# Retention and two gated MLPs on one core: a product kept in PSUM, subtractions moved to GpSimd, stores behind loads, chunks reversed, ten conversions moved up

## Chip, core and metric

One core of one Trainium2 chip. The metric is the device time of one launch in microseconds (us), lower is better. The core has five engines with instruction streams of their own: TensorE (PE, its weight loads PEld), VectorE (DVE), ScalarE (ACT), GpSimd (POOL) and SyncE (SP), which issues most DMAs. Each stream runs in its program order; streams wait for each other by semaphores.

## The reference

Three stages on 4 x 768 tokens of width 512, all in float32:

```python
for t in range(S):                        # retention, 8 heads of 64
    state = gamma * state + outer(k_t, v_t)
    y_t = scale * q_t @ state
h = x @ w_in;  x = (h * cos(h)) @ w_out   # first MLP, 512 -> 2048 -> 512
h = x @ w_in2                             # second MLP, same sizes
g = where(h >= 1, h, where(h <= -1, 0, (h + 1)**2 / 4))
out = g @ w_out2
```

The second MLP's weights arrive as 64-bit words that the kernel converts to float32.

## The kernel before

Every float32 matrix is split into a high part, rounded to the matmul's format, and a low part, the remainder (`high_part`, ACT; `low_part`, POOL). A product is three matmuls: high x high, low x high, high x low.

**Stage 1, first MLP.** Six blocks of 512 tokens; hidden chunks of 128, 16 of them, in two halves of eight (k = 0 and k = 1). A step is `first` (12 matmuls) for one chunk and `second` (12 matmuls) for the chunk three steps earlier; `act` puts the cosine between them. There are 96 steps. Retention runs beside the first 40 of them, block 5 of k = 0 is steps 40 to 47, and k = 1 is steps 48 to 95, eight to a block. When a block is done, `evacuate` (L573) moves four accumulator banks out: even ones with an addition on DVE (L578), odd ones with a copy on ACT (L582) and an addition on POOL (L584). The next block's accumulation takes the same banks.

**Conversion.** `Convert` turns one [128 x 512] weight slice of 64-bit words into float32: load of the raw words (L146), two DVE passes (L153, L156), one on ACT (L161), a DVE pass (L167), a POOL addition (L174). `Conveyor` gives each slice one method per step (`one`, `two`, ...), by lag. The first MLP's slices are converted early. All 32 slices of the second MLP's weights (m = 1) are converted in k = 1, in three steps of four. Two neighbouring slices make a pair: `combine` (L190) forms four half-width sums of it on POOL (L211), and `part` (L213) splits four pieces, the low parts with a DVE subtraction (L225), and stores them on SP at once (L228, L229). From step 68 on, `right_sides(0)` also forms and splits the right-hand sides of stage 2, one closure a step.

**Stage 2, second MLP.** `Products` uses a 2 x 2 block scheme with seven products in place of eight (names 11, t1, 21, t2, 22, t3, t4). Token blocks go in three pairs (p = 0, 1, 2), each with eight groups g % 8, 24 groups in all, with one more pass to drain. In `group` (L859) there are seven segments; each has one input `product` (6 matmuls, L737) of this group and one `output` (6 matmuls, L753) of the group before. The ramp is ACT (`ramp`, `square`) and DVE (`larger`, L789). `add` (L792) adds a finished output bank y to an SBUF accumulator (L823); an output's matmuls wait until its y bank is read. Seven activations per group are split: four direct ones and three differences (t1, L995; t2, L1019; t3, by `minus`), with t4 at L915; low parts are formed by `low` (L779), some on POOL, some on DVE. In segment E the group's d bank receives a sum, its activated value goes to an SBUF tile (`take(g, "22")`).

While p = 0 and p = 1 run, `tick` (L883) calls one closure of `right_sides(p + 1)` five times a group, groups 2 to 6 of each pair: 8 subtractions (L651) and 14 splits (L698), then stores. Two of the five calls use DVE, three POOL. Weight tiles of each group come from DRAM by `load` (L615) on SP, eight a group, and `load_x` fetches the next right-hand sides at a pair's end. When a pair is done, its four accumulators are transposed by DVE (L831) and `send` (L847) issues 16 small DMAs in a row on SP, twice. At the very end two of the four accumulators go by TensorE transposes (L807) and copies (L813, L815), the other two by DVE and 16 small DMAs, half on the ACT queue.

Of the kernel before, what the change touches and what calls it, by code (L numbers as in the profile page):

```python
# [40 lines left out]
def tile_retention_mlp_mlp(  # L41
# [25 lines left out]
    NWARM = 10  # L67

# [5 lines left out]
    yq_d = dram.tile([P, NP, TB], F32, name="yq")  # L74
    w32_d = {
        (m, j, a): dram.tile([P, TB], F32, name=f"w32_{m}_{j}_{a}")
        for m, j, a in [(0, j, a) for j in range(NH, NF) for a in range(2)]
# [56 lines left out]
    class Convert:  # L134
# [4 lines left out]
        def __init__(self, m, j, a, keep):  # L139
            self.m, self.j, self.a, self.keep = m, j, a, keep  # L140

        def load(self, stage):
            self.stage = stage
            self.raw = self.stage.tile([P, TB, 2], I32, tag="raw", name="raw", bufs=3 - self.m)
            src = (w1, w2)[self.m][self.j][:, self.a * TB:(self.a + 1) * TB]
            nc.sync.dma_start(out=self.raw.rearrange("p n w -> p (n w)"), in_=src.bitcast(I32))  # L146

        def one(self):
            ncs, ncf = ((3, 3), (1, 5))[self.m]
# [10 lines left out]
        def two(self):  # L160
            nc.scalar.activation(  # L161
                out=self.s, in_=self.raw[:, :, 0].bitcast(U32), func=AF.Copy, scale=2.0 ** -29
            )

        def three(self):
            f = self.f.bitcast(I32)
# [5 lines left out]
        def four(self):  # L172
            f = self.f.bitcast(I32)
            nc.gpsimd.tensor_tensor(out=f, in0=f, in1=self.s, op=ALU.add)  # L174

        def five(self):
# [3 lines left out]
            elif self.m == 1:  # L180
# [32 lines left out]
        def part(self, n):  # L213
# [9 lines left out]
            for x, o in self.pieces[n]:  # L223
                w = x.shape[-1]
                nc.vector.tensor_tensor(  # L225
                    out=x.bitcast(F32R), in0=x, in1=hi[:, o:o + w].bitcast(F32), op=ALU.subtract
                )
                nc.sync.dma_start(out=to[:, 1, o:o + w], in_=x)  # L228
            nc.sync.dma_start(out=to[:, 0, :], in_=hi[:, :wide[n]].bitcast(F32))  # L229

        def seven(self):
            if self.m == 1 and self.j % 2:
# [3 lines left out]
        def eight(self):  # L236
            if self.m == 1 and self.j % 2:
# [3 lines left out]
    left = {}  # L241

    class Conveyor:
# [20 lines left out]
        def advance(self):  # L264
            if self.late:
                order = (("five", 2), ("one", 1), ("two", 1), ("three", 1), ("four", 1), ("seven", 3), ("eight", 4))
# [321 lines left out]
    class Products:  # L588
# [7 lines left out]
        def __init__(self):  # L596
            self.w, self.x, self.f, self.g = {}, {}, {}, {}
            self.spare, self.ready = [], []
            self.done, self.turned = {}, {}
            self.queue = [[], []]  # L600
            self.eng = nc.gpsimd
# [12 lines left out]

        def load(self, a, g, n):  # L615
            if g >= self.NG:
                return
# [4 lines left out]
            nc.sync.dma_start(out=t.bitcast(F32), in_=wp_d[a][g % NH][n])  # L622
# [13 lines left out]
        def release(self, a, g, n):  # L636
            self.slots[a].append(self.w.pop((a, g, n))[0])
# [43 lines left out]
        def remake(self, p):  # L681
# [12 lines left out]
            def parts(c, q):  # L694
# [3 lines left out]
                self.eng.tensor_tensor(out=lo, in0=x[c][q], in1=hi.bitcast(F32), op=ALU.subtract)  # L698
# [31 lines left out]
        def product(self, g, q, to, begin):  # L730
# [10 lines left out]
            if g % NH == NH - 1:  # L741
                self.free_x(p, q)
                n = 2 * ORDER.index(q)
                for m in range(NP + n, min(NP + n + 2, 14)):
# [15 lines left out]
        def take(self, g, q):  # L760

            if q == "21":
                t = tp.tile([P, TB], F32, tag="r", name="r", bufs=5)
            else:
                nm = {"11": "h6", "t3": "h6", "t1": "l6", "t4": "l6", "22": "h7", "t2": "l7"}[q]
                pool = self.tmp if q == "t3" else wpool[0]
                t = pool.tile([P, TB], F32, tag=f"wo{nm}", name=f"f{q}")
# [20 lines left out]
        def larger(self, r, h):  # L788
            nc.vector.tensor_tensor(out=r, in0=h, in1=r, op=ALU.max)  # L789


        def add(self):  # L792
# [10 lines left out]
            elif fine and final and n == 0:  # L803
                for e in range(2):
                    nc.vector.tensor_tensor(out=a[:, e, :], in0=y[:, e, :], in1=a[:, e, :], op=ALU.add)
                    for i, z in enumerate(self.z[h]):
                        nc.tensor.transpose(z[:, e * P:(e + 1) * P], a[:, e, i * P:(i + 1) * P], self.eye)  # L807
                for i, z in enumerate(self.z[h]):
                    o = tp.tile([P, TB], F32, tag="r", name="o", bufs=5)[:, :2 * P]
                    to = o.rearrange("p (k e b) -> p e k b", k=4, e=2)  # L810
                    src = z.rearrange("p (e k b) -> p e k b", k=4, e=2)
                    if i < 2:
                        nc.vector.tensor_copy(out=to, in_=src)  # L813
                    else:
                        nc.scalar.activation(out=to, in_=src, func=AF.Copy)  # L815
                    t0 = (i * NC + 2 * p) * C
                    rows = out[t0:t0 + C, :].rearrange("t (k x) -> t k x", k=4)
                    (nc.sync, nc.scalar)[h * (i // 2)].dma_start(
                        out=rows[:, :, h * 64:(h + 1) * 64], in_=o.rearrange("p (k x) -> p k x", k=4)
                    )  # L820
# [9 lines left out]
            def turned():  # L830
# [3 lines left out]
                if at in (("22",) if fine else ("12", "21")):  # L834
                    self.send(p, n, fine)

            if fine:
                turned()
            else:
                self.turned[at] = turned  # L840
# [6 lines left out]
        def send(self, p, n, fine):  # L847
# [3 lines left out]
            for k in range(4):  # L851
                src = t[32 * k:32 * (k + 1)].rearrange("p (q c) e -> p q c e", q=NP)
                for q in range(NP):
                    (nc.scalar if fine and q % 2 else nc.sync).dma_start(
                        out=rows[k, :, q, 2 * p + n, :, :], in_=src[:, q]
                    )


        def group(self, g, banks, ends):  # L859
# [3 lines left out]
            if live:  # L863
                a, b, c, d = [bank(i) for i in banks]
# [18 lines left out]
            def tick(eng=nc.gpsimd):  # L883
                if self.ready:
                    self.eng = eng
# [16 lines left out]
            if live:  # L902
                self.product(g, "11", a, True)
            self.add()
            if o:
                self.square(o["r21"])
                self.larger(o["r21"], o["h21"])
            if live:
                s1 = copy(a)
            if o:  # L910
# [5 lines left out]
                self.low(prev, "22")  # L916
# [6 lines left out]
            if live:  # L923
                self.product(g, "t1", b, True)
# [12 lines left out]
            if live:  # L937
                tick(nc.vector)

            if live:  # L940
                self.product(g, "21", c, True)
# [21 lines left out]
            if live:  # L963
                s6 = copy(a)
                self.square(r11)
                self.larger(r11, c)
# [13 lines left out]
            outputs("t3", y0, False)  # L980
            done(2, 2)
# [8 lines left out]
            if live:  # L990
                plus(d, a, s5)
                self.square(r12)
                self.larger(r12, b)
# [6 lines left out]
            outputs("21", y1, True)  # L1000
            done(0, 3)
            if live:
                tick(nc.vector)
            if live and g % NH == NH - 2:
                for n in range(NP):
# [6 lines left out]
            if not fine:  # L1012
                self.add()
# [11 lines left out]
            outputs("t4", y0, False)  # L1025
            if prev >= 0:
                self.release(1, prev, 3)

        def run(self, before):
# [13 lines left out]
            for g in range(self.NG + 1):  # L1043
# [7 lines left out]
                if g == self.NG:  # L1051
                    self.z = [bank(i) for i in banks]
                    self.z = [[t[:, o:o + 2 * P] for t in self.z[2 * h:2 * h + 2] for o in (0, 2 * P)] for h in range(2)]
# [359 lines left out]
```

## Time and profile before

| | |
|---|---|
| median of 3 runs | 1173.91 us (1169.13 to 1176.9) |
| the profiled execution, its own time | 1170.15 us |
| its span | 1168.4 us |
| TensorE busy, of the span | 1098.0 us, 94% |
| VectorE | 891.6 us, 76% |
| ScalarE | 610.4 us, 52% |
| GpSimd | 554.8 us, 47% |
| mean granted TensorE clock | 0.985 |
| chain that ended last | PE 57%, DVE 16%, DMA 9%, issue 7%, POOL 6% |

A busy TensorE is one with matmuls in its pipe, not one at its peak; so the number of matmuls in a stretch is read beside the busy time. The span leaves out what lies around the first and last instruction; here that is 1.75 us.

### The profile page before, as it was taken

Reading aid. Unit: us, or ns where it says so; the run is one execution under the profiler, and the core shown is the slowest. Engines: PE = TensorE matmul, PEld = TensorE weight load, DVE = VectorE, ACT = ScalarE, POOL = GpSimd, SP = SyncE. Lnnn points to the kernel's source line nnn. Section 1 sums busy time; section 2 is a strip of 40 time slices with the busy share of each in tenths; the row PEclk is TensorE's granted clock in tenths of the full one; section 3 lists DMA queues with packets and bytes.
Section 4 is the critical chain, followed back from the end, with each engine's and each line's share of the span. In section 5 each row is a group of like instructions: output and inputs, shape, how many; then the busy total and the mean of one; then the engine's idle time right before and its main releaser. Section 6 shows DMA issues by size and latency. Waiting matters only on the chain.

```text
span 1168.4 us, 16673 instructions
## 1 busy us (share of the span) xinstructions
PE 1098.0 (94%) x5758; PEld 885.6 (76%) x5758; DVE 891.6 (76%) x1149; ACT 610.4 (52%) x1090; POOL 554.8 (47%) x441
## 2 busy tenths in 40 slices
PE   8999999999999999979889998989988989999995
PEld 5787888888888887868778786767776767778883
DVE  6877566654335789798996589888979888988986
ACT  3554233333345545555554575666555666566662
POOL 4735223321045355666662446756336756345542
PEclk9999999999999999989999999999999999999998
DMA  9476375833173878878776676789697889686543
GB/s 359 158 232 271 111 276 191 298 127 144 46 295 122 291 257 273 302 244 303 276 230 245 227 236 226 261 266 394 203 294 235 267 270 393 202 271 199 180 146 81
DMA packets 125909, 274.63 MB, mean 235 GB/s; under 512 B 17152, under 2 KB 46464, under 8 KB 121856
## 3 DMA queue, kind: packets, MB, share of 16 engines
q1 hardware_dynamic: 119152, 254.94, 64.2%
q10 hardware_dynamic: 6672, 18.61, 4.4%
q8 instruction: 46, 0.75, 0.3%
q14 instruction: 39, 0.32, 0.1%
HBM read 192.76 MB, written 80.74 MB: 234 GB/s over the span
## 4 chain that ended last, share of the span: by engine, by line
PE 57%; DVE 16%; DMA 9%; issue 7%; POOL 6%; ACT 4%; SPq 1%; ACTq 0%; DVEq 0%; POOLq 0%
PE b L567 15%; PE b L480 13%; PE b L737 12%; PE y L753 12%; DMA wo<-wp 2%; DMA raw<-in_w 2%; DVE s L225 2%; DVE cf L225 2%; POOL big L698 2%; PE b L359 1%; PE b L411 1%; DVE cf L153 1%; DVE cf L156 1%; DVE b L532 1%; PE b L417 1%
## 5 line engine op out<-in xcount | busy, mean ns | idle before, releaser
L174 POOL TENSOR_TENSOR cf<-cf,cs 128x512 int32<-128x512 int32 x64 | 86.8, 1356 | 187.8 <-DVE cf L167 113.0
L523 DVE SCALAR_TENSOR_TENSOR r<-b,r 128x512 f32<-128x512 f32 x96 | 65.8, 685 | 130.1 <-ACT r L518 130.1
L518 ACT ACTIVATE r<-b 128x512 int32<-128x512 f32 x96 | 56.8, 591 | 192.1 <-PE b L480 165.0
L567 PE MATMUL b<-gh,wo 128*128 128x512 f32 x384 | 102.9, 405 | 17.5 <-DVE o L578 17.5
L823 DVE TENSOR_TENSOR xh<-y,xh 128x1024 f32<-128x1024 f32 x89 | 108.0, 1213 | 7.9 <-PE y L753 7.9
L753 PE MATMUL y<-wi,wo 128*128 128x512 f32 x342 | 91.0, 402 | 13.8 <-issue 6.8
L567 PEld LDWEIGHTS b<-gh,wo 128*128 128x128 f32 x384 | 74.9, 196 | 34.7 <-ACT r L529 19.0
L536 ACT ACTIVATE gh<-b 128x512 fp32r<-128x512 f32 x96 | 57.2, 596 | 80.3 <-DVE b L532 80.2
L881 POOL TENSOR_TENSOR ft<-f,r 128x512 f32<-128x512 f32 x24 | 41.8, 1743 | 116.6 <-DVE f L789 116.6
L737 PE MATMUL b<-wih,wi 128*128 128x512 f32 x352 | 94.7, 391 | 0.7 <-DVE b L873 0.7
L480 PE MATMUL b<-xh,wi 128*128 128x512 f32 x384 | 95.0, 389 | 0.0
L753 PE MATMUL y<-wo,wo 128*128 128x512 f32 x324 | 83.9, 394 | 8.5 <-issue 3.5
L753 PEld LDWEIGHTS y<-wi,wo 128*128 128x128 f32 x342 | 64.5, 192 | 32.8 <-issue 12.7
L823 DVE TENSOR_TENSOR xl<-y,xl 128x1024 f32<-128x1024 f32 x65 | 79.0, 1215 | 12.4 <-PE y L753 12.1
L480 PEld LDWEIGHTS b<-xh,wi 128*128 128x128 f32 x384 | 72.4, 189 | 15.2
L567 PE MATMUL b<-gh,woh 128*128 128x512 f32 x192 | 77.3, 408 | 2.8 <-ACT woh L117 2.8
L753 PEld LDWEIGHTS y<-wo,wo 128*128 128x128 f32 x324 | 59.6, 188 | 26.2 <-issue 5.1
L753 PE MATMUL y<-gh,wo 128*128 128x512 f32 x228 | 71.3, 394 | 7.0 <-issue 3.0
L737 PEld LDWEIGHTS b<-wih,wi 128*128 128x128 f32 x352 | 66.3, 189 | 15.2 <-DVE b L873 1.1
L480 PE MATMUL b<-xh,wih 128*128 128x512 f32 x192 | 75.4, 395 | 1.6 <-ACT wih L117 0.9
L480 PE MATMUL b<-xh,wil 128*128 128x512 f32 x192 | 74.3, 390 | 0.0
L567 PE MATMUL b<-gh,wol 128*128 128x512 f32 x192 | 74.0, 390 | 0.0
(146 smaller groups left out, 2787.3 us busy)
## 6 DMA issues: line engine op xcount, KB each, us to landing
wi<-wp SPq DMA_DIRECT2D x72, 512.0 KB, 4.9
wo<-wp SPq DMA_DIRECT2D x72, 512.0 KB, 5.1
raw<-in_w SPq DMA_DIRECT2D x64, 512.0 KB, 5.3
wp<-whi SPq DMA_DIRECT2D x48, 256.0 KB, 3.0
qk<-in_qk SPq DMA_DIRECT2D x23, 512.0 KB, 7.3
wp<-s SPq DMA_DIRECT2D x32, 256.0 KB, 2.1
xTh<-xh ACTq DMA_DIRECT2D x6, 1024.0 KB, 5.6
xTl<-xl ACTq DMA_DIRECT2D x6, 1024.0 KB, 9.6
```

The lines of the kernel that those rows point to most:

```text
L174: nc.gpsimd.tensor_tensor(out=f, in0=f, in1=self.s, op=ALU.add)
L225: nc.vector.tensor_tensor(out=x.bitcast(F32R), in0=x, in1=hi[:, o:o + w].bitcast(F32), op=ALU.subtract)
L480: nc.tensor.matmul(out=h, lhsT=w[:, c * P:(c + 1) * P], rhs=x[:, c, :], start=(i == 0), stop=(i == len(terms) - 1),)
L518: nc.scalar.activation(out=self.r.bitcast(I32), in_=self.h, func=AF.Identity, scale=INV_2PI, bias=0.25)
L523: nc.vector.scalar_tensor_tensor(out=self.r, in0=self.h, scalar=INV_2PI, in1=self.r.bitcast(I32), op0=ALU.mult, op1=ALU.subtract,)
L536: nc.scalar.activation(out=self.gh, in_=self.h, func=AF.Copy)
L567: nc.tensor.matmul(out=acc[k, b][e], lhsT=w[:, s], rhs=g, start=(begin and i == 0), stop=(last and i == 2),)
L698: self.eng.tensor_tensor(out=lo, in0=x[c][q], in1=hi.bitcast(F32), op=ALU.subtract)
L737: nc.tensor.matmul(out=to, lhsT=w[:, c * P:(c + 1) * P], rhs=x, start=begin and n == 0, stop=n == len(terms) - 1, skip_group_check=not begin,)
L753: nc.tensor.matmul(out=to[:, e, :], lhsT=w[:, e * P:(e + 1) * P], rhs=a, start=begin and m == 0, stop=m == 2, skip_group_check=not begin,)
L823: nc.vector.tensor_tensor(out=a, in0=y, in1=a, op=ALU.add)
L881: nc.gpsimd.tensor_tensor(out=o, in0=x, in1=z, op=ALU.subtract)
```

## The change

- `low_part` on POOL forms the low parts of the converted weights; the stores are collected and issued by `send_parts` after the next step's load; `part` 3 and 0 come with 1 and 2.
- Odd accumulators of k = 1 are added on DVE straight from the bank.
- Three conversions move into the retention stretch, seven into block 5 of k = 0; their float32 result goes to DRAM (ACT queue) and is loaded in k = 1 in place of conversion.
- In stage 2, 22's activated value is written over the d bank. t2 and t3 read it there on DVE; t1, the low parts of t1 and t2 and all ticks are on POOL; the low part of 22 is on DVE.
- p = 1 walks its chunks backwards, so the weights of the last group of a pair are kept for the first of the next.
- Row stores go five per segment. The end uses TensorE transposes for all four accumulators and stores whole rows. One pair of buffers is given from the activations to the right-hand sides.

```diff
+    READY = 10
+    FIRST = 3
...
     def load(self, stage):
+            if self.ready:
+                self.f = self.stage.tile([P, TB], F32, tag="cf", name="cf", bufs=5)
+                nc.sync.dma_start(out=self.f, in_=w32_d[self.m, self.j, self.a])
+                return
...
     def part(self, n):
-                nc.vector.tensor_tensor(
-                    out=x.bitcast(F32R), in0=x, in1=hi[:, o:o + w].bitcast(F32), op=ALU.subtract
-                )
-                nc.sync.dma_start(out=to[:, 1, o:o + w], in_=x)
-            nc.sync.dma_start(out=to[:, 0, :], in_=hi[:, :wide[n]].bitcast(F32))
+                low_part(hi[:, o:o + w], x.bitcast(F32R), x)
+                stores.append((to[:, 1, o:o + w], x))
+            stores.append((to[:, 0, :], hi[:, :wide[n]].bitcast(F32)))
...
+    def send_parts():
+        for o, x in stores:
+            nc.sync.dma_start(out=o, in_=x)
+        stores.clear()
...
     def evacuate(done, n):
-            if e % 2 == 0 and add:
+            if add:
                 nc.vector.tensor_tensor(out=o, in0=a, in1=add.pop(0), op=ALU.add)
...
+        def chunk(self, g):
+            p, l = divmod(g, NH)
+            return NH - 1 - l if p % 2 else l
+        def again(self, g):
+            return g > 0 and g % NH == 0
         def load(self, a, g, n):
-            if g >= self.NG:
+            if g >= self.NG or self.again(g):
                 return
...
         def turn(self):
-            for f in self.queue.pop(0):
+            for f in self.queue.pop(0) + self.rows[:5]:
                 f()
+            del self.rows[:5]
...
         def sums(self, x, *which):
-                self.eng.tensor_tensor(out=x[o], in0=x[a], in1=x[b], op=ALU.subtract)
+                nc.gpsimd.tensor_tensor(out=x[o], in0=x[a], in1=x[b], op=ALU.subtract)
...
         def group(self, g, banks, ends):
-                self.low(prev, "22")
+                self.low(prev, "22", nc.vector)
...
-                self.low(prev, "t2", nc.vector)
+                self.low(prev, "t2")
...
-                nc.vector.tensor_tensor(out=t1, in0=r12, in1=r11, op=ALU.subtract)
+                minus(t1, r12, r11)
                 self.low(g, "11")
-                r22 = self.take(g, "22")
+                r22 = r()
                 self.ramp(r22, d)
...
                 self.square(r22)
-                self.larger(r22, d)
+                self.larger(d, r22, d)
                 self.high(g, "t1")
                 t2 = self.take(g, "t2")
-                nc.vector.tensor_tensor(out=t2, in0=r22, in1=t1, op=ALU.subtract)
-                self.low(g, "t1", nc.vector)
-                minus(self.take(g, "t3"), r22, r12)
+                self.less(t2, d, t1)
+                self.less(self.take(g, "t3"), d, r12)
+                self.low(g, "t1")
+                self.f[g, "22"] = d
...
+        def final(self):
+            a, p, h, n = self.finals.pop(0)
...
+            for e in range(2):
+                for i in range(NP):
+                    nc.tensor.transpose(z[i][:, e * P:(e + 1) * P], a[:, e, i * P:(i + 1) * P], self.eye)
...
+            for i in range(NP):
+                t0 = (i * NC + 2 * p + n) * C
+                (nc.sync, nc.scalar)[i // 2].dma_start(out=out[t0:t0 + C, :], in_=self.out[n][:, i, :])
...
     def run():
-                now = 5 <= i < 12 if i < 2 * NH else (i < 3 * NH + 4 or i % 2) and bool(todo)
+                now = 5 <= i < 12 if i < 2 * NH else (i < 3 * NH + 4 or i % 2 or i > 33) and bool(todo)
...
-                conv.start(todo.pop(0) if todo and k == 1 and l % 4 != 3 else None, stage)
+                conv.start(todo.pop(0) if todo and (l < 7 if k == 0 else l % 4 != 3) else None, stage)
                 first(k, b, j, 4 + i % 4)
+                send_parts()
```

## Rows read from the trace of the kernel before

**Rows 1.** Windows, stage 1: length, busy us (x instructions) per engine, clock, DMA share, GB/s.
```profile
310.90:354.40 43.50, 43.50 (x194) 36.02 (x193) 16.76 (x26) 21.46 (x40) 15.30 (x12) 1.00 0.55 206
397.90:441.40 43.50, 43.50 (x194) 36.02 (x193) 36.10 (x49) 20.36 (x40) 23.70 (x21) 1.00 0.78 279
441.40:488.00 46.60, 43.87 (x194) 36.02 (x193) 39.44 (x60) 25.27 (x47) 23.47 (x22) 1.00 0.90 307
488.00:541.40 53.40, 46.24 (x194) 37.71 (x193) 50.40 (x61) 28.77 (x55) 35.90 (x32) 0.90 0.74 249
541.40:590.40 49.00, 45.25 (x194) 37.05 (x193) 44.82 (x57) 26.46 (x50) 31.22 (x26) 0.97 0.82 279
590.40:640.50 50.10, 46.27 (x194) 37.75 (x193) 39.07 (x55) 24.84 (x48) 21.59 (x20) 0.93 0.69 235
```

**Rows 2.** Waits, whole span: engine, line, awaited; total us, times, longest.
```profile
PE b L567 <- DVE o L578: 17.5, 4, 7.2
```

**Rows 3.** Windows, stage 2, four groups each, columns PE, PEld, DVE, ACT, POOL.
```profile
697.40:785.70 88.30, 79.25 (x338) 62.20 (x337) 76.22 (x77) 56.56 (x100) 58.69 (x42) 1.00 0.76 250
785.70:872.40 86.70, 80.23 (x338) 63.29 (x337) 73.42 (x81) 52.53 (x91) 39.14 (x28) 0.98 0.85 293
872.40:960.70 88.30, 79.27 (x338) 62.21 (x337) 76.25 (x77) 56.62 (x100) 58.73 (x42) 1.00 0.79 261
960.70:1044.90 84.20, 78.80 (x338) 62.20 (x337) 73.39 (x81) 52.53 (x91) 39.15 (x28) 1.00 0.86 298
1044.90:1121.00 76.10, 76.10 (x338) 63.00 (x336) 65.73 (x73) 51.55 (x89) 39.22 (x28) 1.00 0.62 195
```

**Rows 4.** Timeline in a group with ticks: start us, us, engine, line, operation.
```profile
722.00 1.73 POOL L881 TENSOR_TENSOR ft<-f,r 128x512 f32<-128x512 f32 x1 [2.42 <-DVE f L789]
722.50 1.79 DVE L779 TENSOR_TENSOR gl<-ft,gh 128x512 fp32r<-128x512 f32 x1
...
724.21 1.21 DVE L823 TENSOR_TENSOR xl<-y,xl 128x1024 f32<-128x1024 f32 x1
...
725.49 0.30 PEld L753 LDWEIGHTS y<-gh,wo 128*128 128x128 f32 x2 [1.57 <-issue]
```

**Rows 5.** Timeline behind the first pair's end, SP queue and TensorE.
```profile
848.48 8.58 SPq L854 DMA_DIRECT2D out<-big  x16
...
861.22 1.19 PE L753 MATMUL y<-wi,wo 128*128 128x512 f32 x2 [3.08 <-DMA wo<-wp]
```

**Rows 6.** Timeline of the end.
```profile
1155.13 0.40 PE L753 MATMUL y<-gl,wo 128*128 128x512 f32 x1
...
1160.35 0.66 ACT L815 ACTIVATE o<-b 128x256 f32<-128x256 f32 x2 [14.52 <-DMA out<-big]
```

**Rows 7.** Groups by line and form, whole span: busy us, mean ns, idle before.
```profile
L174 POOL TENSOR_TENSOR cf<-cf,cs 128x512 int32<-128x512 int32 x64 | 86.8, 1356 | 187.8 <-DVE cf L167 113.0 <-ACT whi L117 22.6 <-issue 16.0
L167 DVE SCALAR_TENSOR_TENSOR cf<-raw,cf 128x512 int32<-128x512 int32 x64 | 58.8, 920 | 1.3
L225 DVE TENSOR_TENSOR s<-s,whi 128x512 fp32r<-128x512 f32 x32 | 37.0, 1196 | 5.2 <-ACT whi L117 4.5 <-issue 0.7
L225 DVE TENSOR_TENSOR cf<-cf,whi 128x256 fp32r<-128x256 f32 x32 | 22.3, 736 | 2.1 <-ACT whi L117 2.1
L120 POOL TENSOR_TENSOR wo<-wo 128x512 fp32r<-128x512 f32 x8 | 10.3, 1293 | 0.9 <-ACT wo L117 0.9
L211 POOL TENSOR_TENSOR s<-cf,s 128x256 f32<-128x256 f32 x16 | 12.2, 762 | 1.3
L995 DVE TENSOR_TENSOR ft<-r,f 128x512 f32<-128x512 f32 x24 | 25.0, 1042 | 2.4
L779 DVE TENSOR_TENSOR wi<-ft,wi 128x512 fp32r<-128x512 f32 x17 | 23.8, 1402 | 0.0
L789 DVE TENSOR_TENSOR r<-b,r 128x512 f32<-128x512 f32 x48 | 32.6, 680 | 6.3 <-ACT r L786 6.3
```

**Rows 8.** Waits of the SP queue, whole span.
```profile
SPq L228 <- DVE s L225: 92.4, 27, 10.6
```

More of the change, by code (lines that the diff above doesn't have):

```diff
@@ L134, in tile_retention_mlp_mlp, with __init__ @@
     class Convert:
[L139 to L140 removed]
+        def __init__(self, m, j, a, keep, late=False, ready=False, store=False):
+            self.m, self.j, self.a, self.keep, self.late, self.ready = m, j, a, keep, late, ready
+            self.store = store or not late
         def load(self, stage):
             self.stage = stage
[L144 removed]
+            if self.ready:
+                self.f = self.stage.tile([P, TB], F32, tag="cf", name="cf", bufs=5)
+                nc.sync.dma_start(out=self.f, in_=w32_d[self.m, self.j, self.a])
+                return
+            self.raw = self.stage.tile([P, TB, 2], I32, tag="raw", name="raw", bufs=3 - self.late)
             src = (w1, w2)[self.m][self.j][:, self.a * TB:(self.a + 1) * TB]
@@ L148, in one @@
         def one(self):
-            ncs, ncf = ((3, 3), (1, 5))[self.m]
+            if self.ready:
+                return
+            ncs, ncf = ((3, 3), (1, 5))[self.late]
             self.s = self.stage.tile([P, TB], I32, tag="cs", name="cs", bufs=ncs)
@@ L160, in two @@
         def two(self):
+            if self.ready:
+                return
             nc.scalar.activation(
@@ L165, in three @@
         def three(self):
+            if self.ready:
+                return
             f = self.f.bitcast(I32)
@@ L172, in four @@
         def four(self):
+            if self.ready:
+                return
             f = self.f.bitcast(I32)
@@ L236, in eight @@
         def eight(self):
-            if self.m == 1 and self.j % 2:
+            if not self.store and self.j % 2:
                 self.part(3)
                 self.part(0)
-    left = {}
+    left, stores = {}, []
+    def send_parts():
+        for o, x in stores:
+            nc.sync.dma_start(out=o, in_=x)
+        stores.clear()
     class Conveyor:
@@ L265, in advance @@
             if self.late:
-                order = (("five", 2), ("one", 1), ("two", 1), ("three", 1), ("four", 1), ("seven", 3), ("eight", 4))
+                order = (("five", 2), ("one", 1), ("two", 1), ("three", 1), ("four", 1), ("seven", 3), ("eight", 3))
             else:
@@ L598, in __init__ @@
             self.spare, self.ready = [], []
-            self.done, self.turned = {}, {}
+            self.done, self.turned, self.out = {}, {}, {}
+            self.rows, self.finals = [], []
             self.queue = [[], []]
-            self.eng = nc.gpsimd
             self.NG = NB // 2 * NH
@@ L636, in release @@
         def release(self, a, g, n):
-            self.slots[a].append(self.w.pop((a, g, n))[0])
+            t = self.w.pop((a, g, n))
+            if self.again(g + 1) and g + 1 < self.NG:
+                self.w[a, g + 1, n] = t
+            else:
+                self.slots[a].append(t[0])
         def right_sides(self, p):
@@ L743, in product @@
                 n = 2 * ORDER.index(q)
-                for m in range(NP + n, min(NP + n + 2, 14)):
+                for m in range(NP + 1 + n, min(NP + n + 3, 14)):
                     self.load_x(p + 1, m)
@@ L802, in add @@
                 nc.vector.tensor_copy(out=a, in_=y)
-            elif fine and final and n == 0:
+            elif fine and final:
                 for e in range(2):
                     nc.vector.tensor_tensor(out=a[:, e, :], in0=y[:, e, :], in1=a[:, e, :], op=ALU.add)
[L806 to L820, printed above, removed]
+                self.finals.append((a, p, h, n))
                 return
@@ L902, in group @@
             if live:
+                a = bank(banks[0])
                 self.product(g, "11", a, True)
@@ L923, in group @@
             if live:
+                b = bank(banks[1])
                 self.product(g, "t1", b, True)
@@ L937, in group @@
             if live:
-                tick(nc.vector)
+                tick()
             if live:
+                c = bank(banks[2])
                 self.product(g, "21", c, True)
@@ L1000, in group @@
             outputs("21", y1, True)
+            self.final()
             done(0, 3)
             if live:
-                tick(nc.vector)
+                tick()
             if live and g % NH == NH - 2:
-                for n in range(NP):
+                for n in range(NP + 1):
                     self.load_x(g // NH + 1, n)
@@ L1052, in run @@
                     self.z = [bank(i) for i in banks]
-                    self.z = [[t[:, o:o + 2 * P] for t in self.z[2 * h:2 * h + 2] for o in (0, 2 * P)] for h in range(2)]
+                    self.nz = 0
                 self.group(g, banks, ends)
@@ L1061, in run @@
                     )
-                    self.pairs += [("wo", n) for n in range(NH + NP + 1, NF)]
+                    self.pairs += [("wo", n) for n in range(NH + NP + 1, NF - 1)]
+                    self.spare.append(self.pair(("wo", NF - 1)))
                     t = [xpool.tile([P, NP, TB], F32R, tag=t, name=t) for t in ("xh", "xl")]
```

83 lines of the change are left out of this document (49 added, 34 removed).

## The prediction, made before the result was known

> **What bounds the kernel now.** I read the windows cut at the blocks of stage 1 and at every four groups of stage 2 first, since the page's shares of busy time mix stages; then the waits of TensorE, then the timeline before single gaps, and last the groups by line, for prices.
>
> A block of eight steps takes 43.50 us when TensorE never waits, with 194 matmuls in it (the first two of [rows 1]). The last four blocks have as many matmuls and take 46.60, 53.40, 49.00 and 50.10 us: 3.1 + 9.9 + 5.5 + 6.6 = 25.1 us lost. In the worst of them the granted clock is 0.90; between the two levels, 2.4 and 1.2 GHz, that is 10.7 us at the lower one, so about half of its 9.9 us is the price of the slow clock after a stop, not of the stop. VectorE is busy 50.40 of 53.40 us there, and the stop itself is TensorE waiting for the evacuation's addition on VectorE, 17.5 us in four waits [rows 2]. VectorE has fallen behind, and the bill is presented at the block's end, when its banks are needed.
>
> Four groups of stage 2 take 76.10 us when TensorE never waits (338 matmuls, 2.72 us a segment; the last of [rows 3]). The four others with that count take 88.30, 86.70, 88.30 and 84.20: 12.2 + 10.6 + 12.2 + 8.1 = 43.1 us lost. The two of 88.30 are those with ticks; VectorE is busy 76.2 us in them, GpSimd 58.7. A typical gap [rows 4]: a GpSimd subtraction starts at 722.00; VectorE's subtraction of two SBUF tiles starts at 722.50 and takes 1.79 us, ending 0.56 us after GpSimd's; the accumulation from y behind it ends at 725.42, and TensorE's load of output weights starts at 725.49. The row says "issue", but the reader is to see that VectorE's queue was the last to finish. In the two windows at the ends of pairs part of the loss is of another kind: 16 row stores hold the SP queue for 8.58 us, and TensorE then waits 3.08 us for a weight tile [rows 5].
>
> The end: the last output matmul is done at 1155.5, the span ends at 1168.4, 12.9 us later, and ScalarE's copies start only at 1160.35, behind the stores on its queue [rows 6].
>
> So at most 25.1 + 43.1 us are in the two stages and some 8 of the 12.9 us in the end, since a last addition, transposes, copies and stores have to remain.
>
> **The change, part by part.**
>
> *Low parts of the weights to GpSimd, odd evacuations to VectorE.* VectorE loses 37.0 + 22.3 us and eight more subtractions of full width at 1.196, 69 us over 16 pairs, 4.3 a pair, 13 a block of three pairs [rows 7]. It gains two additions a block at 0.680. The worst block falls from 50.4 to about 39 busy us; a block in which it was busy 36.10 lost nothing (the second of [rows 1]). GpSimd gains, a pair, 2.5 full subtractions and two half ones: 2.5 x 1.293 + 2 x 0.762 = 4.8, 14.3 a block, and loses two additions (2.6) [rows 7]. Its busy time in the third to fifth block goes from 23.5, 35.9, 31.2 to 35.2, 47.6, 42.9 against 43.5. No stretch of this trace has GpSimd above two thirds, so this is the unknown of the change. Between "all 25.1 us come back" and "none do, GpSimd gates where VectorE did" I take what the sums show: 4 us over in the fourth block, 1 us in its neighbours, and 2 us of lower clock; 18 us come back.
>
> *Stores behind the next load.* The SP queue spent 92.4 us waiting for those subtractions, with the next raw load behind them [rows 8]. Afterwards the stores wait for GpSimd, and behind them are the load after next, the evacuation's stores and the fetch of right-hand sides. A raw load gets one more step, 5.4 us, of slack; I count this into the 18 and nothing on its own.
>
> *Ten conversions earlier.* One costs VectorE at most three passes of 0.920 and GpSimd 1.356 [rows 7]. Seven in the last block of k = 0 raise VectorE from 16.76 to at most 36.1 us of 43.5, which was seen to be free, GpSimd from 15.3 to 24.8 [rows 1]. Three more lie beside the retention, where VectorE has as much room: nothing. If that cover were gone they would cost up to 28 us of VectorE time. The k = 1 blocks that lose them (the first two) lost nothing before, so the gain is nothing either, but the queues enter the third block empty. Ten stores and ten loads of float32 slices are added, 5 MB; the kept weights take away 7 MB.
>
> *22 in PSUM, t1 and low parts on GpSimd, ticks on GpSimd.* Per group VectorE gives up t1 (1.042) and two low parts (about 1.40 each) and takes t3 and the low part of 22 from the bank, at the price of an operation with a bank operand, 0.680 [rows 7]; t2 stays. In tick groups some 1.6 subtractions more go, at 0.68 to 1.4. That is 19.1 - 3.8 - 1.6 + 1.4, about 15 us of 19.0. GpSimd does one operation more, and in tick groups those 1.6: 14.7 + 2.6 x 1.293 = 18.0 at today's durations [rows 3, 7]. They fall if the durations do: of VectorE's operations in the group loop none has two SBUF operands any more, and the 1.73 us of [rows 4] is 0.44 above the 1.293 of one alone. I take 17, again below the segment rate and again above anything shown. The added wait is t2 on VectorE for t1 on GpSimd; queued behind it are t3, the next accumulation and the release of a y bank, which TensorE needs. t1 is issued one segment, 2.72 us, ahead, which covers it when GpSimd has at most one operation in front. Bounds: all 24.4 us of tick groups return, or the new wait costs as much as the old and 8 us on top. I take 17 returned, since the nearest row (the last of [rows 3], VectorE at 65.73 of 76.10 busy and no loss) shows that the loop tolerates one engine at 86%.
>
> The trace shows two neighbours slowed together when both read two SBUF operands [rows 4]. The Trainium skill, page "SBUF — State Buffer", section "SBUF: two separate sides", says why: VectorE and GpSimd share a port pair that one holds for a whole instruction while the other blocks, and a VectorE operation with one bank operand is not among those that take it. By that rule GpSimd's operations in stage 2 fall to 1.29 each, 16 us a tick group, and the stall is gone; by today's durations alone it is 18.
>
> *Chunks reversed, row stores five a segment, spare pair.* Sixteen weight loads vanish at the two turns, just where the next right-hand sides are loaded. 16 stores take 8.58 us of SP [rows 5], 0.54 each; five are 2.7 us, a whole segment, so weight loads still slip by some 0.7 us a segment over seven segments, but none waits 8.58 us. A tile is fetched most of a group ahead. Of 18.7 us in the two windows I take 11 back: the 3.08 with its slow clock, once, and the doubled operations; between 3 and 18.7.
>
> *The end.* Two transposes on VectorE, 16 small stores and the delay of ScalarE's copies go; 16 TensorE transposes come, beside waits. After 1155.5 remain two additions, transposes, copies, issue and landing: about 9 us. 4 us return; between -1 and 8.
>
> Sum: 18 + 17 + 11 + 4 = 50 us from 1170.15, the profiled execution's own time: 1120. That execution lies 3.8 us below the median of the runs shown and inside their spread; I put half of this on it: **1122 us**.
>
> **Rivals.**
>
> *A. GpSimd becomes the bound.* For it: 47.6 of 43.5 us in one block, 17 to 18 of 19.0 in tick groups, and waits of its own for ScalarE's high parts. Against it: with work queued, waits overlap. At 1.73 us for each of 12.4 operations a tick group takes 21.5, no less than 22.1 now: nothing of the 24.4, some 12 of stage 1, 9 of the turns, 4 of the end: 25 us, 1147. The Trainium skill, "GPSIMD Engine Reference", section "Engine selection", advises against GpSimd for two-input work as about 2x slower; the trace agrees for work undisturbed, 1.293 against 0.680 [rows 7], and by that rule this rival is the result.
>
> *B. The SP queue takes over.* Five row stores fill a segment, the weight loads behind them come late and the 3.08 us wait recurs with its clock: the 11 us are not gained: 1133. Against it: sixteen loads fewer at that place.
>
> *C. Slower: t1's wait.* Where a tick's two sums stand before t1 in GpSimd's queue, t1 is 2 x 1.29 + 1.29 late; past the 2.72 us of slack VectorE stops, its accumulations stop, and low parts of t1 and t2 come late the same way. If each of them adds the 3.2 us by which GpSimd's three operations exceed one of 0.68, that is 6.4 us on ten tick groups, 64 us, against 24.4 removed: 40 us lost, 26 kept elsewhere: 1184. It decides from about 5 us a tick group on.
>
> *D. No change.* The stops move to another engine in both stages and the gains of the turns are eaten: 1170.
>
> **How the numbers follow.** A measurement of this kernel tells about 1%, 12 us, from no change. Forecast 0.64, own range 1104 to 1136; A 0.18; B 0.06; C 0.06; D 0.06. The range reaches down to nearly all of the losses returned (25.1 + 43.1 + 4 gives 1098; 1102 taken) and up over A with its bounds to 1158; C, D and a little of both ends are outside. Faster by over 1%: forecast, B and nearly all of A, 0.87. Within 1%: D and a rest of A, 0.07. Slower: C, 0.06.
>
> **What would show it.** Right: third to sixth blocks of k = 1 at 44 to 48 us, the waits for L578's successor under 6 us in total; GpSimd over 40 us busy in a block; tick windows at 77 to 82 us with GpSimd operations near 1.3; no wait of TensorE for weights at the turns; under 10 us after the last output matmul. Wrong: VectorE's idle time before t2 put down to GpSimd's t1; ScalarE waiting for GpSimd's sums in k = 1; TensorE waiting for wp tiles. The forecast fails if GpSimd is late by more than a segment for long stretches.

## The result

The changed kernel takes 1119.42 us, median of the runs timed first, against 1172.3: ratio 0.9543, 95% interval 0.9499 to 0.9587, so 53 us less. Timed again, in five executions, it takes 1116.68 (ratio 0.9542, 0.9521 to 0.9562). The forecast was 1122 in a range of 1102 to 1158. The execution profiled with the first timing was disturbed (2796 us, the common matmul forms at 828 ns on the mean where they take about 390 otherwise) and is left out of the ratios; without it the first median is 1118.84. The rows below are of the same kernel in the later run, an execution of 1114.82 us.

| | before | after |
|---|---|---|
| profiled execution, its span | 1170.15, 1168.4 us | 1114.82, 1113.0 us |
| TensorE busy | 1098.0 us (94%) | 1086.1 us (98%) |
| VectorE busy | 891.6 us | 776.6 us |
| GpSimd busy | 554.8 us | 631.3 us |
| last four blocks of k = 1, sum (174.0 without waits) | 199.1 | 181.6 |
| sixteen groups with losses, sum (304.4 without waits) | 347.5 | 312.5 |

The last two lines are sums of windows: of [rows 1], [rows 3], and of the answer below, with the same columns (length; busy us and count of PE, PEld, DVE, ACT, POOL; clock, DMA share, GB/s). The first four are blocks three to six of k = 1. Then come four times four groups: the first and third hold nearly all ticks ("tick windows"), the second and fourth lie around the ends of pairs ("turn windows"). The last is four groups that waited for nothing before either.

```profile
441.70:485.20 43.50, 43.50 (x194) 36.02 (x193) 29.62 (x45) 22.63 (x43) 33.72 (x33) 1.00 0.88 314
485.20:529.40 44.20, 44.17 (x194) 35.70 (x193) 33.52 (x44) 25.80 (x50) 41.35 (x39) 1.00 0.78 279
529.40:579.80 50.40, 46.12 (x194) 37.66 (x193) 38.51 (x49) 26.84 (x50) 46.53 (x43) 0.93 0.83 293
579.80:623.30 43.50, 43.50 (x194) 35.92 (x193) 27.30 (x40) 22.88 (x44) 28.12 (x29) 1.00 0.70 242
680.80:757.80 77.00, 76.52 (x338) 63.07 (x337) 57.88 (x67) 56.34 (x100) 65.74 (x53) 1.00 0.84 284
757.80:834.40 76.60, 76.39 (x338) 62.94 (x337) 64.62 (x74) 52.11 (x92) 43.07 (x35) 1.00 0.81 273
834.40:915.80 81.40, 78.64 (x338) 63.99 (x337) 57.91 (x67) 55.91 (x100) 65.31 (x52) 0.98 0.85 293
915.80:993.30 77.50, 76.84 (x338) 62.83 (x337) 64.68 (x75) 52.50 (x92) 43.49 (x36) 1.00 0.82 275
993.30:1069.50 76.20, 76.20 (x338) 63.12 (x337) 59.48 (x69) 51.04 (x89) 40.53 (x33) 1.00 0.61 200
```

The reader is to see the exchange of VectorE and GpSimd: in the tick windows VectorE goes from 76.2 to 57.9 us, GpSimd from 58.7 to 65.7, and TensorE loses 0.9 and 5.3 us where it lost 12.2 twice. In stage 1 one block of four still loses, the fifth, 6.9 us, with GpSimd at 46.5 of 50.4.

The groups by line of the changed kernel, against [rows 7]; the last column is idle time before and who ended it:

```profile
L809 POOL TENSOR_TENSOR gl<-ft,gh 128x512 fp32r<-128x512 f32 x56 | 71.8, 1301 | 1.3 <-ACT gh L120 1.3
L920 POOL TENSOR_TENSOR ft<-r,f 128x512 f32<-128x512 f32 x24 | 31.2, 1298 | 140.7 <-PE y L784 93.4 <-DVE r L819 47.3
L954 POOL TENSOR_TENSOR ft<-f,ft 128x512 f32<-128x512 f32 x23 | 30.0, 1303 | 21.0 <-DVE f L819 21.0
L822 DVE TENSOR_TENSOR ft<-b,ft 128x512 f32<-128x512 f32 x24 | 16.6, 692 | 2.5
```

t1 (L920, formerly DVE at 1042 ns), t4 (L954) and the low parts of full width take GpSimd 1.30 us with little scatter; t2 (L822) follows on VectorE after 2.5 us of idle time in all, so the wait that rival C feared hardly exists.

What is left in the fifth block is rival A on a small scale. The timeline there (start, length, engine, operation):

```profile
544.43 0.63 ACT L120 ACTIVATE wih<-wih 128x512 fp32r<-128x512 f32 x1 [4.20 <-POOL wih L682]
...
545.74 1.43 POOL L227 TENSOR_TENSOR s<-cf 128x256 f32<-128x256 f32 x2
547.14 0.73 POOL L227 TENSOR_TENSOR s<-s,cf 128x256 f32<-128x256 f32 x1
...
547.90 0.63 ACT L120 ACTIVATE whi<-s 128x512 fp32r<-128x512 f32 x1 [2.28 <-POOL s L227]
...
550.17 0.57 ACT L537 ACTIVATE r<-b 128x512 int32<-128x512 f32 x1
...
550.78 0.69 DVE L542 SCALAR_TENSOR_TENSOR r<-b,r 128x512 f32<-128x512 f32 x1 [6.92 <-ACT r L537]
...
551.99 2.48 DVE L597 TENSOR_TENSOR o<-b,xh 128x512 f32<-128x512 f32 x4
...
552.81 3.75 PE L586 MATMUL b<-gh,wo 128*128 128x512 f32 x8 [4.28 <-DVE o L597]
```

ScalarE waits for GpSimd twice, 4.20 us for a difference of right-hand sides (L682) and 2.28 us for half sums (L227), each time to make a high part; its next step's rounding (L537) stands behind. VectorE waits 6.92 us for that, and the evacuation behind it holds TensorE. The engine named at TensorE's wait is VectorE, as before; the late one is GpSimd. At the end, the last copies start at 1107.53 and the last store is issued at 1107.95, against copies that start from 1160.35 to 1164.85 before ([rows 6] and the first line here):

```profile
1164.85 0.38 ACT L815 ACTIVATE o<-b 128x256 f32<-128x256 f32 x1 [0.71 <-DMA out<-o]
```

```profile
1107.53 0.66 ACT L893 ACTIVATE big<-b 128x256 f32<-128x256 f32 x2 [1.71 <-PE b L884]
1107.95 0.82 ACTq L898 DMA_DIRECT2D out<-big  x2
```

From the end of the last output matmul (1103.9) to the end of the span are 9.1 us.

### The profile page after: what moved, and what is told of

Its sections match the earlier page's. It is cut to its first block, busy times and chain, and to the rows that moved or that the text cites. A ratio compares the mean times of both kernels' runs of the same rounds, so it can differ in the third digit from the quotient of the medians.

```text
span 2794.4 us, 16654 instructions
## 1 busy us (share of the span) xinstructions
PE 2785.6 (100%) x5774; PEld 1677.8 (60%) x5774; DVE 763.1 (27%) x1053; ACT 606.0 (22%) x1082; POOL 614.7 (22%) x541
## 4 chain that ended last, share of the span: by engine, by line
PE 100%; DVE 0%; ACT 0%; issue 0%
PE b L499 25%; PE b L586 25%; PE b L768 21%; PE y L784 21%; PE b L378 2%; PE b L436 2%; PE b L430 2%; PE b L401 1%; PE b L884 0%; PE b L1157 0%; DVE big L891 0%; DVE b L912 0%; DVE xl L838 0%; ACT xh L120 0%; ACT big L893 0%
## 5 line engine op out<-in xcount | busy, mean ns | idle before, releaser
L537 ACT ACTIVATE r<-b 128x512 int32<-128x512 f32 x96 | 57.3, 597 | 1087.2 <-PE b L499 1046.7
L586 PE MATMUL b<-gh,wo 128*128 128x512 f32 x384 | 244.0, 828 | 0.0
L499 PE MATMUL b<-xh,wi 128*128 128x512 f32 x384 | 239.9, 828 | 0.0
L784 PE MATMUL y<-wi,wo 128*128 128x512 f32 x360 | 228.0, 827 | 0.0
L190 POOL TENSOR_TENSOR cf<-cf,cs 128x512 int32<-128x512 int32 x64 | 81.7, 1276 | 608.5 <-DVE cf L181 403.6
L768 PE MATMUL b<-wih,wi 128*128 128x512 f32 x320 | 211.2, 828 | 0.0
L784 PE MATMUL y<-gh,wo 128*128 128x512 f32 x272 | 193.7, 829 | 0.0
L499 PE MATMUL b<-xh,wil 128*128 128x512 f32 x192 | 159.7, 836 | 0.0
L768 PEld LDWEIGHTS b<-wih,wi 128*128 128x128 f32 x320 | 113.3, 354 | 77.2 <-issue 72.3
L920 POOL TENSOR_TENSOR ft<-r,f 128x512 f32<-128x512 f32 x24 | 30.7, 1277 | 581.1 <-DVE r L819 581.1
L586 PE MATMUL b<-gh,wol 128*128 128x512 f32 x192 | 156.5, 823 | 0.0
L586 PE MATMUL b<-gh,woh 128*128 128x512 f32 x192 | 154.9, 813 | 0.0
L784 PEld LDWEIGHTS y<-gh,wo 128*128 128x128 f32 x272 | 95.5, 351 | 66.9 <-issue 66.9
L586 PE MATMUL b<-gl,woh 128*128 128x512 f32 x192 | 130.3, 834 | 0.0
L586 PE MATMUL b<-gl,wo 128*128 128x512 f32 x192 | 129.7, 828 | 0.0
```

The costliest lines, as they stand in the source:

```text
L499: nc.tensor.matmul(out=h, lhsT=w[:, c * P:(c + 1) * P], rhs=x[:, c, :], start=(i == 0), stop=(i == len(terms) - 1),)
L537: nc.scalar.activation(out=self.r.bitcast(I32), in_=self.h, func=AF.Identity, scale=INV_2PI, bias=0.25)
L586: nc.tensor.matmul(out=acc[k, b][e], lhsT=w[:, s], rhs=g, start=(begin and i == 0), stop=(last and i == 2),)
L768: nc.tensor.matmul(out=to, lhsT=w[:, c * P:(c + 1) * P], rhs=x, start=begin and n == 0, stop=n == len(terms) - 1, skip_group_check=not begin,)
L784: nc.tensor.matmul(out=to[:, e, :], lhsT=w[:, e * P:(e + 1) * P], rhs=a, start=begin and m == 0, stop=m == 2, skip_group_check=not begin,)
L920: nc.gpsimd.tensor_tensor(out=o, in0=x, in1=z, op=ALU.subtract)
```

## The experiments

Ratios are to the kernel before, timed on the same chip. "Stage 1" is the sum of the last four blocks of k = 1 (before 199.1, changed 181.6), "ticks" and "turns" those of the two tick and the two turn windows of stage 2 (before 176.6 and 170.9, changed 158.4 and 154.1). These sums are of one execution each; a second one of the changed kernel has 182.0 in stage 1.

| run | median us | ratio, interval | stage 1 | ticks | turns |
|---|---|---|---|---|---|
| changed, again | 1116.68 | 0.9542 (0.9521 to 0.9562) | 181.6 | 158.4 | 154.1 |
| weight low parts on VectorE | 1119.96 | 0.9561 (0.9544 to 0.9578) | 185.4 | | |
| stores at once | 1137.80 | 0.9717 (0.9697 to 0.9737) | 204.3 | | |
| no early conversions | 1121.99 | 0.9578 (0.9547 to 0.9608) | 182.1 | | |
| before + stores behind | 1173.23 | 1.0007 (0.9990 to 1.0025) | 197.1 | | |
| before + stores behind + lows on GpSimd | 1169.94 | 0.9990 (0.9975 to 1.0005) | 194.3 | | |
| chunks forward | 1125.37 | 0.9614 (0.9585 to 0.9642) | | 155.4 | 163.6 |
| t1 and two low parts on VectorE | 1125.66 | 0.9609 (0.9581 to 0.9637) | | 158.0 | 162.2 |
| two ticks of five on VectorE | 1128.12 | 0.9625 (0.9611 to 0.9639) | | 166.0 | 155.2 |
| both of these | 1146.53 | 0.9792 (0.9775 to 0.9809) | | 178.1 | 164.1 |
| even ticks, early store of xhi | 1116.76 | 0.9545 (0.9523 to 0.9567) | 187.2 | 154.1 | 154.9 |

**The changed kernel again**, twice, without an edit. The first was a single execution: 1113.96 us.

> The changed kernel as it is, for a trace of an ordinary execution. Theory (VectorE relieved, GpSimd holds): blocks three to six of k = 1 at 44 to 48 us, windows of four groups with ticks at 77 to 82 us, under 10 us after the last output matmul. Rival A (GpSimd is now the bound): the fourth and fifth block at 48 us or more with GpSimd over 95% busy, tick windows at 84 us or more.

> The changed kernel timed beside the next one: both theories 1114 to 1120 us.

The windows were as the theory had them (77 to 82 us with ticks, blocks at 48 or less), but for the fifth block, 49.8 and 50.4 us in the two runs.

**Weight low parts back on VectorE.**

```diff
-                low_part(hi[:, o:o + w], x.bitcast(F32R), x)
+                nc.vector.tensor_tensor(out=x.bitcast(F32R), in0=x, in1=hi[:, o:o + w].bitcast(F32), op=ALU.subtract)
```

> The low parts of the second MLP's weights go back to VectorE, all else as changed. Theory: VectorE falls behind again at block ends of k = 1, but less than before, since ten conversions and the stores are better placed: 8 to 16 us slower than the changed kernel. Rival A (GpSimd was the bound in k = 1): no slower, or faster by up to 5 us. Rival S (the stores' place did it): under 4 us slower.

3.3 us slower against 8 to 16 forecast, so rival S's "under 4" is what came. Stage 1 loses 3.8 us more, and the intervals of the two ratios overlap. The move that the prediction put first is worth little when the rest of the change is in place.

**Stores at once**, on SP ahead of the next load, low parts still on GpSimd.

```diff
-                stores.append((to[:, 1, o:o + w], x))
-            stores.append((to[:, 0, :], hi[:, :wide[n]].bitcast(F32)))
+                nc.sync.dma_start(out=to[:, 1, o:o + w], in_=x)
+            nc.sync.dma_start(out=to[:, 0, :], in_=hi[:, :wide[n]].bitcast(F32))
```

> The stores of the weight parts are issued at once, ahead of the next step's load, all else as changed. Theory: VectorE has room, so a load that is late by a GpSimd subtraction is still in time: within 4 us of the changed kernel. Rival S (the queue order is what mattered): 8 to 16 us slower.

21 us slower, beyond even rival S's 8 to 16. Waits of VectorE between 440 and 650 us (engine, line, awaited; total, times, longest), with stores at once:

```profile
DVE cf L163 <- DMA raw<-in_w: 36.9, 8, 9.5
```

and in the changed kernel, same view:

```profile
DVE cf L163 <- DMA raw<-in_w: 3.3, 3, 1.2
```

The waits of the SP queue for the low parts, whole span, are these, first with stores at once, then in the changed kernel:

```profile
SPq L242 <- POOL s L123: 123.5, 30, 13.9
```

```profile
SPq L259 <- POOL s L123: 82.6, 30, 8.5
```

So the queue stands at stores whose low parts GpSimd has not made in either kernel; the edit decides whether the next raw load stands behind them. With stores at once the raw load is late, VectorE stops at the conversion's first pass, and everything in its queue with it. VectorE is busy only 33.1 us of the 57.1 of the worst block: not loaded, but held.

**No early conversions.**

```diff
-    READY = 10
-    FIRST = 3
+    READY = 0
+    FIRST = 0
...
-                conv.start(todo.pop(0) if todo and (l < 7 if k == 0 else l % 4 != 3) else None, stage)
+                conv.start(todo.pop(0) if todo and k == 1 and l % 4 != 3 else None, stage)
```

> No conversion moves ahead: all 32 are converted in k = 1. Theory: the first two blocks of k = 1 have room for what comes back (20.9 us of VectorE time, 13.6 of GpSimd's), and the last four are unchanged: within 5 us of the changed kernel. Rival (the early ones bought the gain, GpSimd being short): 8 to 20 us slower.

Stage 1 is the same to 0.5 us: the ten conversions bring nothing there that can be measured. In all it is 5.3 us slower, just past the forecast 5, with overlapping intervals. In the profiled execution 3.8 us of that lie ahead of the third block of k = 1, which starts at 445.5 in place of 441.7; whether the edit or the execution did that is not shown.

**The kernel before with the stores behind the load**, low parts on VectorE as before: in `part`, `stores.append(...)` for the two `dma_start`, and `send_parts()` behind `first`.

> The kernel before with one part of the change: the stores of the weight parts behind the next step's load. Theory as it stands after the run that stored at once: the place in the SP queue gives most of stage 1's gain, 10 to 18 us faster than the kernel before. Rival (VectorE's own load stopped TensorE, as predicted): under 5 us faster, VectorE still the one that L567 waits for.

No faster. The theory made after the run above, that the place of the stores was the cause, fell as well: it costs 21 us to put them in front when GpSimd makes the low parts, and brings 2 us of stage 1 to put them behind when VectorE does.

**The kernel before with both**, stores behind and low parts on GpSimd (the first diff the other way round, on top of the last).

> The kernel before with two parts of the change: the weight parts' low parts on GpSimd, and their stores behind the next load. No early conversions, odd banks evacuated by ScalarE and GpSimd as before, stage 2 as before. Theory J (the two only work together): stage 1 loses 8 to 12 us in place of 25, 13 to 17 us faster than the kernel before. Rival V (the odd evacuation on VectorE is a part of it): under 8 us faster, since GpSimd also carries the odd additions.

Again no faster in all, as rival V had it, and 4.8 us less in stage 1. (In the profiled executions of these two kernels the third block starts 2.1 and 2.8 us later than in the kernel before, at 441.4; why is not shown.) TensorE's waits at L567's successor, first in the kernel with the stores alone, then with both:

```profile
PE b L572 <- DVE o L583: 14.4, 4, 4.5
```

```profile
PE b L570 <- ACT o L585: 12.5, 4, 4.5
```

Four waits at four block ends in each. With the low parts gone from VectorE the wait goes over to ScalarE's copy of the odd banks. This and the run without early conversions, at 182.1, differ in stage 1 by two things alone: odd banks added on VectorE straight from the bank, and pieces 3 and 0 made a step earlier. Together they are worth 12.2 us, once the other two edits are in. The name at the wait points to the first; the two were not tried apart.

**Chunks forward.**

```diff
-            return NH - 1 - l if p % 2 else l
+            return l
...
-            return g > 0 and g % NH == 0
+            return False
```

> All pairs walk their chunks forwards, so every group loads its weights; all else as changed. Theory: the sixteen loads come back where the row stores are, but five a segment leave room between: 2 to 8 us slower than the changed kernel, with TensorE waiting for weight tiles in groups 8 to 11 or 16 to 19. Rival (the loss at the turns was VectorE and GpSimd in each other's way): under 2 us.

8.7 us slower, a little more than expected, and where expected: the turn windows go to 81.7 and 81.9 us, 9.5 us more in sum, and TensorE waits for weight tiles; in the changed kernel its only such wait is one of 0.5 us:

```profile
PE b L768 <- DMA wi<-wp: 6.4, 2, 3.2
```

**t1 and the low parts of t1 and t2 on VectorE.**

```diff
-                minus(t1, r12, r11)
+                self.less(t1, r12, r11)
...
-                self.low(prev, "t2")
+                self.low(prev, "t2", nc.vector)
...
-                self.low(g, "t1")
+                self.low(g, "t1", nc.vector)
```

> t1 and the low parts of t1 and t2 go back to VectorE; 22 stays in PSUM and the ticks stay on GpSimd. Theory (both engines held each other up): the operations with two SBUF operands are back, 1.0 to 1.8 us each where GpSimd is busy, tick windows lose 6 to 17 us in all. Rival (the ticks alone made the difference): under 4 us slower. Rival C (t1's wait on GpSimd costs): faster by 1 to 5 us.

9 us slower, but not where expected: the tick windows are the same in sum (158.0 against 158.4), and the turn windows, where VectorE also has the transposes of the accumulators, take 8.1 us more, with VectorE busy 74.9 of 81.4 us in the first. The groups by line show two neighbours stretched again, a low part on VectorE and one on GpSimd:

```profile
L809 DVE TENSOR_TENSOR gl<-ft,gh 128x512 fp32r<-128x512 f32 x28 | 40.7, 1452 | 0.0
...
L809 POOL TENSOR_TENSOR wi<-f,wi 128x512 fp32r<-128x512 f32 x24 | 37.7, 1570 | 46.9 <-ACT wi L120 46.9
```

In the changed kernel the GpSimd operation takes 1.30; it reads and writes the same tiles in both. Not every such operation is stretched: t1 itself reads two SBUF tiles on VectorE in this run too and takes 0.69, and 21 low parts of other forms take 0.68.

```profile
L822 DVE TENSOR_TENSOR ft<-r,f 128x512 f32<-128x512 f32 x24 | 16.6, 692 | 0.9
```

**Two ticks of five on VectorE**: `tick(nc.vector)` behind t1 and 21, with `self.eng` in `sums` and `parts`, as before.

> Two of the five ticks of a group go back to VectorE, all else as changed. Theory: VectorE rises by 1.6 operations a tick group to about 17 of 19.0 us and meets GpSimd again: 3 to 10 us slower. Rival (t1 and the low parts were all of it): under 2 us. Rival A (GpSimd is short): 1 to 3 us faster.

11.4 us slower, just past the expected bound, and 7.6 us of it in the tick windows.

**Both.**

> Both stage 2 edits that were undone singly are undone together: t1, the low parts of t1 and t2 and two ticks of five on VectorE; 22 stays in PSUM. Theory (each fills the room that the other left on VectorE): more than the sum of the two, 20 to 30 us slower than the changed kernel. Rival (they are separate costs): the sum, 14 to 18 us.

29.9 us slower, against 9.0 + 11.4 for the two alone. Of the 35.0 us that the sixteen groups won, 29.7 are lost again. The surplus over the sum lies in the tick windows: 19.7 us more there, where the two edits alone cost nothing and 7.6; in the turn windows it is 10.0, against 8.1 + 1.1. In the tick windows the edits share one margin. Either one alone leaves VectorE 64.5 to 67.2 us busy, in windows of 78.7 to 84.6 us; both leave it at 76.2 of 90.1 and 77.2 of 88.0, as in the kernel before (76.2 of 88.3). So t1, the two low parts and the ticks are all of the tick windows' gain, with 22 in PSUM still in place. That part was not undone on its own; what it is worth is not shown.

**Even ticks, early store.** In k = 1 no closure of the right-hand sides in the two steps with a pair's low parts; in stage 2 the store of a high part at once.

```diff
+                nc.sync.dma_start(out=xb_d[p, q, c][0], in_=hi.bitcast(F32))
...
-                if ready:
+                if ready and l not in (1, 7):
```

> The changed kernel with two edits: in k = 1 no right-hand-side closure in the steps in which GpSimd has a pair's low parts (l = 1 and 7), so the work spreads to the last block; in stage 2 the store of a high part is issued with its tick, not a segment later. Theory: the fifth block of k = 1 loses 1 to 2 us in place of 6, the groups in which ScalarE waited for that store under 1 in place of 2.5: 5 to 9 us faster than the changed kernel. Rival (the fifth block's loss comes from DMA, the store's from the rings): within 2 us of it.

No faster in all, by two effects that cancel. The fifth block falls to 45.1, but the sixth, which had waited for nothing, now takes 53.8:

```profile
530.20:575.30 45.10, 44.25 (x194) 35.80 (x193) 28.81 (x42) 21.79 (x41) 34.64 (x33) 1.00 0.75 265
575.30:629.10 53.80, 46.99 (x194) 37.68 (x193) 35.07 (x47) 28.34 (x53) 40.55 (x40) 0.94 0.70 245
```

The work was moved and the stop with it: TensorE's wait of 6.2 us there again comes after a wait of ScalarE for GpSimd's half sums, 3.7 us. Stage 2 is better: the second tick window takes 76.5 us, which was 81.4, and the sixteen groups 309.0 in place of 312.5. In the changed kernel ScalarE waits in that window four times for the store of a high part, 8.0 us in all, and TensorE 1.9 us for ScalarE; here ScalarE's waits are 1.5 us and TensorE has none. The early store alone, without the moved closures, was not run. No version tried beats the changed kernel.

## Why the prediction was right, and where it was not

**The sum.** 18 + 17 + 11 + 4 = 50 was forecast against the profiled execution, and 55.3 came (1170.15 to 1114.82). By the windows: stage 1 17.5 (199.1 to 181.6), tick windows 18.2 (176.6 to 158.4), turns 16.8 (170.9 to 154.1), the end 3.8 (12.9 to 9.1). Three terms are right in size; the turns were mis-sized at 11 for 16.8. In the rivals, C's 1184 puts 26 us as kept elsewhere, where the sum's own terms make 18 + 11 + 4 = 33; nothing of the outcome hangs on it.

**Stage 1: right in size, wrong in its working.** The prediction said that VectorE's load stopped TensorE, that the low parts were the cure, and that the stores' place counted for nothing on its own. So that 18 came out is in part luck. Undone, the low parts cost 3 us and the stores 21. Done alone, the stores bring nothing measurable in total time; with the low parts added, 4.8 us of stage 1; with odd banks and pieces 3 and 0 as well, 17.0. In these runs TensorE's wait at a block's end went from VectorE's addition to ScalarE's copy, and in the changed kernel to a chain that starts at GpSimd: a part that relieved one engine handed the wait to the next. That GpSimd-made low parts need the stores behind the load was in the prediction as "behind them are the load after next", but as a risk without a price; its price is 36.9 us of VectorE's waiting where 3.3 are left otherwise. Early conversions at nothing in stage 1: confirmed.

**GpSimd near its limit.** The prediction had 7 us stay lost in stage 1, 4 of them in the fourth block; 7.6 did, nearly all in the fifth. Its "No stretch of this trace has GpSimd above two thirds" missed one at the start, 29 to 58 us, with GpSimd busy 22.3 of 29. Forecast 47.6 and 42.9 us in the fourth and fifth block; measured 41.4 and 46.5. The block over 43.5 is the fifth, it loses 6.9, and the timeline has GpSimd's sums at the head of the chain. One sign that the prediction named for being wrong, ScalarE waiting for GpSimd's sums in k = 1, is there; rival A holds for one block in four.

**Stage 2: right in the tick windows.** 17 was forecast to return, 18.2 did, and the two edits undone together take 19.7 away. VectorE was forecast at about 15 us a tick group and is at 57.9 / 4 = 14.5; GpSimd at 17 and is at 16.4. t1's wait stayed within its slack. By the rule of the Trainium skill, page "SBUF — State Buffer", section "SBUF: two separate sides" (one of the two engines blocks while the other holds the shared ports; a VectorE operation with one bank operand is not among those that take them), GpSimd's operations would fall to 1.29: the trace agrees with 1.30, and with 1.57 for one form when two-operand work was given back to VectorE. The rule of the Trainium skill, page "GPSIMD Engine Reference", section "Engine selection", against two-input work on GpSimd holds for the price, 1.30 against 0.69, and not for the time of this kernel, in which the slower engine had the room.

**Turns.** The kept weights are 9.5 us of it by the run that undid them. Another share came with the relief of VectorE: with t1 and low parts back on it, the turn windows take 81.4 and 80.8 us, 8.1 more, though the weights were kept. The two make 17.6, about the 16.8 that came. The prediction counted the wait for weights with its slow clock and "the doubled operations" and put them too low. Row stores at five a segment were in every run of the changed kernel, so their share is not shown.

**The end.** 4 forecast, 3.8 measured. No run undid it by itself.

## What to carry to other kernels

Where several in-order engines form a chain, price a part of a change by what it does with the others in place and without them: here two parts without effect on the total belong to a gain of 17 us in one stage, and two that cost 9 and 11 us when undone cost 30 together. When a producer moves to a slower engine, look at once at the DMA queue that waits for its result, and at the loads behind. An engine that is slower per operation can still be the better place when the faster one is the bound: here 1.30 us on GpSimd in place of 0.69 to 1.45 on VectorE. That the operations left behind read a PSUM bank may have helped; it was not tried apart.

## What the hardware showed beyond expectation

With t1 and two low parts back on VectorE, one form of low part, a VectorE subtraction of two SBUF tiles, took 1.45 us on the mean and 1.71 at most, where others of its kind in the same run took 0.68; a low part on GpSimd took 1.57, not 1.30. The loss is on both sides, 0.76 and 0.27 us on the mean, but not at every such operation. With one operand in a bank VectorE stays at 0.69 (L822), also in the tick window in which GpSimd is busy 85% of the time.
